# Transposes moved between TensorE and the DMA queue in a fused linear-attention and SwiGLU kernel

## The chip, the cores and the metric

The kernel runs on one core of one Trainium2 chip. The metric is the device time in microseconds of one execution; the median of several runs counts. A core has five engines with queues of their own: TensorE (PE in the profile; its weight loads are PEld), VectorE (DVE), ScalarE (ACT), GpSimd (POOL) and SyncE (SP), which here only issues DMAs. An engine takes its instructions strictly in the order in which the program lists them, so an instruction that waits holds up all that stands behind it on its engine.

## The reference

Eight batches of eight heads with 576 positions of 64 features go through a linear attention with cosine weights; its output, 4608 tokens of 512 features, goes through a normalized SwiGLU layer.

```python
def phi(x, c, s):
    r = np.maximum(x, 0.0)
    return np.concatenate([r * c, r * s], axis=-1)
q_p, k_p = phi(q, cos_w, sin_w), phi(k, cos_w, sin_w)
kv = np.einsum('bhsf,bhsd->bhfd', k_p, v)
z = np.sum(k_p, axis=2)
num = np.einsum('bhsf,bhfd->bhsd', q_p, kv)
den = np.einsum('bhsf,bhf->bhs', q_p, z)[..., None] + 1e-06
x = (num / den)                       # tokens x 512 after a transpose
xn = x / np.sqrt(np.mean(x * x, axis=-1, keepdims=True) + 1e-06) * rms_g
g, val = xn @ w_gate, xn @ w_val      # 512 -> 1536
out = (g / (1.0 + np.exp(-g)) * val) @ w_out
```

## The kernel before

**Blocks and tiles.** The tokens of a batch make a block: 512 of its 576 positions in four x tiles of 128 tokens. The last 64 positions of two batches each ("tails") make one further tile, and the four such tiles are block 8. The blocks of the SwiGLU layer run in the order 0, 1, 2, 3, 4, 5, 6, 8, 7. For a block there are twelve steps (n = 0 to 11), each with four matmuls of 512 columns for the gate into a bank `psG` and four for the value into a bank `psV` (`half_mm`, L528). `gval_h` then takes the silu of the gate on ScalarE (L547) and the product with the value on VectorE into `hT` (L548). Four output steps (n = 12 to 15) follow, of twelve matmuls each into `psC` (L551); their copies and stores are `out_store` (L562).

**From attention to an x tile.** For each batch, k, v and q are loaded into a ring of five `raw` buffers (`load_kv`, `load_q`; L109, L114, L123). `k_phi` and `q_phi` (L281 on ScalarE, L283 on VectorE) apply relu and the cosine or sine; `v_cast` makes v bf16; `kvz_pe` forms kv and z and `kvz_evac` saves them. The phi of q is transposed to `qpT`, by TensorE for batches 0 and 1 (`q_tr_pe`, L335), by a DMA transpose from SyncE for the others (`q_tr_dma`, L318). `nd_pe` (L421; `nd0_pe`, L430, in batch 0) forms numerator and denominator of one x tile in `psA`; `nd_post` on VectorE divides (reciprocal and L471); `x_sq` squares and sums on ScalarE (L487) and takes the power on GpSimd (L492, `rs`); `x_norm` on VectorE gives the normalized tile `xn` (L499). The tile must then be transposed into `xnT`, of which there are two, for even and odd blocks. For batches 0 and 1 TensorE does it: `x_tr_pe` (L518) makes four 128x128 transposes into a PSUM bank, and `x_tr_evac` copies that bank to `xnT` (L277 on VectorE, L275 on ScalarE). For the other batches SyncE issues a DMA transpose (`x_tr_dma`, L512).

**Queues and order.** The order on each engine is written out by hand. For the steady part it is a table: `at(block, step, where, f, ...)` puts a call into a slot, and `run` makes the calls of a slot before the matmuls of the step ("pe"), after them ("pre"), after the products ("post"), or amid the output matmuls ("mid"). Batch b+1's attention is thus made within block b. GpSimd issues the weight loads and, early in the program, loads of k, v and q; SyncE the others, with all stores and DMA transposes.

**The start of block 0.** To begin before all four x tiles exist, eight gate-and-value steps of block 0 are cut into eight `units`. A unit is (first tile, last tile, first n, last n): units 0 to 3 hold one tile and four n (sixteen matmuls of 128 columns for the gate, sixteen for the value), units 4 to 7 hold tiles 2 and 3 together and two n (eight matmuls of 256 columns for each). Unit i uses bank `psG[i % 2]` and `psV[i % 2]`; `unit_mm` (L618) makes its matmuls, `unit_silu` (L629) and `unit_h` (L633) its silu and product. `filler` (L573) multiplies zeros where TensorE would stand idle. The order written out there, around the change:

```python
    filler(2, psG[1])
    unit_mm(0, wg, by_rows=True)
    x_tr_pe(0, 1, psC[0])
    ...
    unit_mm(2, wg)
    x_tr_pe(0, 2, psC[1])
    x_tr_evac(V, 0, 2, psC[1])
    unit_silu(2)
    unit_h(0)
    unit_mm(3, wg)
    x_tr_pe(0, 3, psC[0])
    x_tr_evac(V, 0, 3, psC[0])
    unit_silu(3)
    unit_h(1)
    unit_mm(4, wg)
```

**The output stage of block 0.** `out_first` makes the 48 output matmuls of block 0, and amid them the four x tiles of batch 1 at the places of the table `X1`. For tile j that table lists where its `nd_pe`, its `x_norm` and its transpose go.

Of the kernel before, what the change touches and what calls it, by code (L numbers as in the profile page):

```python
# [17 lines left out]
def kernel(  # L18
# [11 lines left out]
    nc = tc.nc  # L30
# [3 lines left out]
    P = 128  # L34
# [6 lines left out]
    NDT = DM // P  # L41
# [5 lines left out]
    V, A, G = nc.vector, nc.scalar, nc.gpsimd  # L47
# [10 lines left out]
    psG = [ps.tile([P, 512], FP32, name=f"psG{i}") for i in range(2)]  # L58
    psV = [ps.tile([P, 512], FP32, name=f"psV{i}") for i in range(2)]
    psC = [ps.tile([P, 512], FP32, name=f"psC{i}") for i in range(2)]  # L60
# [66 lines left out]

    rqt = {}

    def load_q_tails(pair):  # L130
        rqt[pair] = two.tile([P, H, D], FP32, name="rqt", tag="rqt")
        for i in range(2):
            nc.sync.dma_start(
                out=rqt[pair][64 * i : 64 * i + 64, :, :],
                in_=q[2 * pair + i, :, 512:576, :].rearrange("h s d -> s h d"),
            )
# [31 lines left out]
    wg = one.tile([P, NDT, DFF], BF16, name="wg")  # L168
    wv = one.tile([P, NDT, DFF], BF16, name="wv")
# [42 lines left out]
    part, left = [], 1e-6  # L212
# [53 lines left out]
    xnT = [one.tile([P, NDT, TB], BF16, name=f"xnT{i}") for i in range(2)]  # L266
# [6 lines left out]
    def copy(eng, o, i):  # L273
        if eng is A:
            A.copy(out=o, in_=i)  # L275
        else:
            eng.tensor_copy(out=o, in_=i)  # L277
# [201 lines left out]
    def nd_post(b, j):  # L479
        nd_rec(b, j)  # L480
        nd_div(b, j)
# [22 lines left out]
    def x_dst(b, j):  # L504
        if j == 4:
            t, col = xnT_tail, b // 2
        else:
            t, col = xnT_of(b), j
        return t[:, :, col * P : (col + 1) * P]
# [4 lines left out]
    def x_tr_pe(b, j, bank, ts=(0, NDT)):  # L514
        xn = xn_of[(b, j)]
        dst = bank.bitcast(BF16).rearrange("p (t s) -> p t s", s=P)
        for t in range(*ts):
            nc.tensor.transpose(dst[:, t, :], xn[:, t * P : (t + 1) * P], ident[:, :])  # L518

    def x_tr_evac(eng, b, j, bank, ts=(0, NDT)):  # L520
        dst = bank.bitcast(BF16).rearrange("p (t s) -> p t s", s=P)
        copy(eng, x_dst(b, j)[:, ts[0] : ts[1], :], dst[:, ts[0] : ts[1], :])
# [48 lines left out]
    def filler(n, bank):  # L571
        for _ in range(n):
            nc.tensor.matmul(  # L573
                bank[:, :], lhsT=warm[:, 0:P], rhs=warm[:, :], start=True, stop=True
            )
# [30 lines left out]
    units = [(j, j + 1, 4 * i, 4 * i + 4) for i in range(2) for j in range(2)]  # L606
    units += [(2, 4, n, n + 2) for n in range(0, 8, 2)]
    sg_of = {}

    def unit_mm(i, w, by_rows=False):  # L610
        j0, j1, n0, n1 = units[i]
        bank = (psG if w is wg else psV)[i % 2]
        width = (j1 - j0) * P
        todo = [(n, t) for n in range(n0, n1) for t in range(NDT)]
        if by_rows:
            todo = [(n, t) for t in range(NDT) for n in range(n0, n1)]
        for n, t in todo:
            nc.tensor.matmul(  # L618
                bank[:, (n - n0) * width : (n - n0 + 1) * width],
                lhsT=w[:, t, n * P : (n + 1) * P],  # L620
                rhs=xnT[0][:, t, j0 * P : j1 * P],
                start=(t == 0 and (n == n0 or not by_rows)),
                stop=(t == NDT - 1 and (n == n1 - 1 or not by_rows)),
                skip_group_check=by_rows,
            )

    def unit_silu(i):
        sg_of[i] = four.tile([P, TB], FP32, name="sg", tag="sg")
        A.activation(out=sg_of[i][:, :], in_=psG[i % 2][:, 0:TB], func=AF.Silu)  # L629

    def unit_h(i):
        j0, j1, n0, n1 = units[i]
        V.tensor_tensor(  # L633
            out=hT[:, n0:n1, j0 * P : j1 * P],
            in0=psV[i % 2][:, 0:TB].rearrange("p (n s) -> p n s", n=n1 - n0),
            in1=sg_of[i][:, :].rearrange("p (n s) -> p n s", n=n1 - n0), op=ALU.mult,
        )
# [32 lines left out]
    q_tr_evac(A, 0, 3, qbank[3])  # L670
    x_norm(0, 1)
    nd_post(0, 2)
    filler(2, psG[1])
    unit_mm(0, wg, by_rows=True)
    x_tr_pe(0, 1, psC[0])
    x_tr_evac(V, 0, 1, psC[0])
    unit_mm(0, wv)
    x_sq(0, 2)
    load_wo(0, 4)
    unit_silu(0)  # L680
    nd0_pe(3)
    nd_post(0, 3)
    x_norm(0, 2)
    unit_mm(1, wg)
    unit_mm(1, wv)
    x_sq(0, 3)
# [6 lines left out]
    x_tr_evac(V, 0, 2, psC[1])  # L693
    unit_silu(2)
    unit_h(0)
    unit_mm(3, wg)
    x_tr_pe(0, 3, psC[0])
    x_tr_evac(V, 0, 3, psC[0])
    unit_silu(3)
    unit_h(1)  # L700
    unit_mm(4, wg)
    for i in range(2, 4):
        unit_mm(i, wv)
        unit_h(i)
    unit_silu(4)
    unit_mm(5, wg)
    unit_mm(4, wv)
    unit_silu(5)
# [4 lines left out]
    def at(blk, n, where, f, *args):  # L713
        slots.setdefault((blk, n), {}).setdefault(where, []).append((f, args))
# [19 lines left out]
    at(0, 10, "post", load_kv, "v", 2, (0, HP), G)  # L734
    at(0, 12, "pe", kvz_pe, 1)
    at(0, 12, "pe", kvz_evac, A, 1)
    at(0, 11, "post", load_q, 2, (0, 4), G)

    def x_tr(b, j, bank):
        x_tr_pe(b, j, bank)  # L740
# [3 lines left out]
    X1 = (  # L744
        ((12, "mid"), (13, "pe"), (14, "pe")),
        ((13, "pe"), (13, "mid"), (14, "mid")),
        ((13, "mid"), (14, "pe"), (15, "pe")),
        ((14, "pe"), (14, "mid"), (15, "mid")),
    )
# [3 lines left out]
        if j:  # L753
            at(0, *X1[j - 1][1], x_norm, 1, j - 1)
    at(0, *X1[3][1], x_norm, 1, 3)
    for j in range(4):
        at(0, *X1[j][2], x_tr, 1, j, psV[j % 2])
    for nb in range(2, B):
        b = nb - 1
        first = nb == 2  # L760
# [16 lines left out]
        for j in range(4):  # L777
            n = ((6, 8, 10, 12) if first else (4, 6, 8, 10))[j]
# [6 lines left out]
    for pair in range(4):  # L785
        b = 2 * pair or 3
        if pair == 0:
            at(1, 15, "post", load_q_tails, 0)
        at(b, 3, "post", q_tails_phi, V, pair, 0)
        at(b, 3, "post", q_tails_phi, A, pair, 1)  # L790
        at(b, 3, "post", q_tails_tr_dma, pair)
        at(b, 12, "pe", nd_tails_pe, pair)
        at(b, 12, "pre", nd_post, 2 * pair + 1, 4)
        at(b, 12, "post", x_sq, 2 * pair + 1, 4)
        at(b, 13, "post", x_norm, 2 * pair + 1, 4)
        at(b, 13, "post", x_tr_dma, 2 * pair + 1, 4)
    for nb in range(3, B):
        b = nb - 2
        late = b == 1
        at(b, 0, "post", load_kv, "k", nb)  # L800
        at(b, 5 if late else 3, "post", load_kv, "v", nb)
        at(b, 8 if late else 6, "post", load_q, nb)
        if nb % 2 == 1:
            at(b, 9, "post", load_q_tails, nb // 2)

    def gval_step(blk, n):
        run(blk, n, "pe")
# [86 lines left out]
```

## Time and profile before

| what | value |
|---|---|
| median of 3 runs | 325.12 us (324.64 to 325.19) |
| the profiled execution's own time | 324.66 us |
| its span, first to last instruction | 322.9 us |
| mean granted TensorE clock | 0.999 |
| busy share of the span: PE, PEld, DVE, ACT, POOL | 98%, 51%, 57%, 51%, 13% |
| DMA traffic | 53.37 MB, 165 GB/s on the mean |

All times inside an execution are counted from the start of the span, which is 1.8 us shorter than the execution's own time. A row of the timeline gives the start, the length, the engine with the source line, the operation, the tile written and the tiles read, their shapes, how many instructions were merged, and in brackets the idle time ahead and what ended it. A DMA's row is its issue (SPq for SyncE's queue); the data move later. Matmuls overlap: the length of a row holds the last one's way through the array, so the cost of a group is read from one start to the next.

In the 40 slices of the span the DMA engines are at 5 to 9 tenths in the first 27, and the granted TensorE clock is in the top tenth in every one.

### The profile page before, as it was taken

To read this page: it belongs to the slowest core of one execution; us is meant where nothing else is said; L and a number is where in the kernel's file an instruction comes from. 1 tells how busy PE (TensorE), PEld (TensorE's weight loads), DVE (VectorE), ACT (ScalarE), POOL (GpSimd) and SP (SyncE) were. 2 spreads that over 40 slices of the span, in tenths; PEclk is the share of its full clock that TensorE was granted. 3 is DMA by queue.
4 is the path that set the end of the run, shared out by engine and by line. 5 is a ranking of instruction groups with operands and counts; after the bars stand their busy time and mean duration, and the time that the engine had idled before them with its cause. 6 is when DMAs were issued, how large, how long until landed. Compare 5 with 4: busy or idle time off the path is not lost.

```text
span 322.9 us, 6078 instructions
## 1 busy us (share of the span) xinstructions
PE 315.6 (98%) x2312; PEld 163.5 (51%) x2348; DVE 185.5 (57%) x380; ACT 164.9 (51%) x319; POOL 40.6 (13%) x78
## 2 busy tenths in 40 slices
PE   8999999999999999999999999999999999999996
PEld 3688565544454445444544445444544444444444
DVE  8875958767636773676457745781577034204410
ACT  5664766744665457445754575446644333223321
POOL 9771302001001100011001000110011000000000
PEclk9999999999999999999999999999999999999999
DMA  7999996999789966998699959994822300041002
GB/s 229 233 266 272 283 327 240 230 200 240 149 156 232 234 190 161 195 233 202 175 198 214 210 148 207 202 217 141 119 49 48 117 32 0 2 98 31 3 32 97
DMA packets 77627, 53.37 MB, mean 165 GB/s; under 512 B 50410, under 2 KB 71326, under 8 KB 77598
## 3 DMA queue, kind: packets, MB, share of 16 engines
q1 hardware_dynamic: 70374, 39.81, 58.2%
q0 software_dynamic: 7216, 13.17, 16.5%
q8 instruction: 18, 0.29, 0.4%
q14 instruction: 11, 0.09, 0.1%
q10 hardware_dynamic: 8, 0.00, 0.0%
HBM read 37.83 MB, written 9.44 MB: 146 GB/s over the span
## 4 chain that ended last, share of the span: by engine, by line
PE 93%; DMA 2%; DVE 2%; issue 1%; POOL 0%; ACT 0%; ACTq 0%; POOLq 0%
PE psV L528 27%; PE psC L551 27%; PE psG L528 26%; PE psA L421 2%; DMA raw<-in_q_dram 2%; PE psG L551 2%; PE psV L618 2%; PE psA L359 2%; PE psG L618 1%; PE psA L366 1%; DVE xn L499 1%; PE psV L335 0%; PE psA L446 0%; DVE xt L471 0%; PE psG L402 0%
## 5 line engine op out<-in xcount | busy, mean ns | idle before, releaser
L548 DVE TENSOR_TENSOR hT<-psV,sg 128x512 bf16<-128x512 f32 x100 | 68.9, 689 | 102.1 <-PE psV L528 65.0
L547 ACT ACTIVATE sg<-psG 128x512 f32<-128x512 f32 x100 | 59.2, 592 | 62.5 <-PE psG L528 54.6
L528 PE MATMUL psV<-xnT,wv 128*128 128x512 bf16 x345 | 89.8, 379 | 0.6
L528 PE MATMUL psG<-xnT,wg 128*128 128x512 bf16 x338 | 88.6, 379 | 0.6 <-issue 0.2
L551 PE MATMUL psC<-wo,hT 128*128 128x512 bf16 (+1 forms) x398 | 88.6, 376 | 0.5
L551 PEld LDWEIGHTS <-hT 128*128 128x128 bf16 x456 | 42.9, 98 | 47.1
L528 PEld LDWEIGHTS <-wv 128*128 128x128 bf16 x400 | 39.1, 98 | 47.2
L528 PEld LDWEIGHTS <-wg 128*128 128x128 bf16 x400 | 37.0, 98 | 39.8
L492 POOL TENSOR_TENSOR rs<-ms,mhalf 128x1 f32<-128x1 f32 x36 | 19.8, 550 | 195.6 <-ACT scr L487 195.6
L275 ACT COPY osb<-psC 128x512 f32<-128x512 f32 x32 | 18.7, 585 | 50.0 <-PE psC L551 46.1
L487 ACT ACTIVATE scr<-xt 128x513 bf16<-128x513 f32 x36 | 22.8, 635 | 25.2 <-DVE xt L471 25.1
L499 DVE SCALAR_TENSOR_TENSOR xn<-xt,rs,gb 128x512 bf16<-128x512 f32 (+1 forms) x37 | 26.9, 730 | 10.3 <-POOL rs L492 10.3
L281 ACT ACTIVATE kp<-raw,tab 128x256 bf16<-128x256 f32 (+2 forms) x51 | 28.8, 607 | 2.3 <-DMA raw<-in_k_dram 2.3
L471 DVE TENSOR_TENSOR xt<-psA,rec 128x512 f32<-128x512 f32 x36 | 24.9, 692 | 1.2
L281 ACT ACTIVATE qp<-raw,tab 128x512 bf16<-128x512 f32 x32 | 22.6, 714 | 0.8 <-DMA raw<-in_q_dram 0.8
L283 DVE TENSOR_SCALAR kp<-raw,tab 128x256 bf16<-128x256 f32 (+2 forms) x53 | 20.4, 429 | 0.3 <-DMA raw<-in_k_dram 0.3
L283 DVE TENSOR_SCALAR qp<-raw,tab 128x512 bf16<-128x512 f32 x31 | 15.5, 506 | 0.3 <-DMA raw<-in_q_dram 0.3
L421 PEld LDWEIGHTS <-qpT 128*128 128x128 bf16 x224 | 10.5, 97 | 6.6 <-issue 0.5
L528 PE MATMUL psV<-xnT_tail,wv 128*128 128x512 bf16 x48 | 12.3, 379 | 0.1
L528 PE MATMUL psG<-xnT_tail,wg 128*128 128x512 bf16 x46 | 12.1, 379 | 0.1
L421 PE MATMUL psA<-kvzs,qpT 128*128 128x65 bf16 x224 | 11.4, 193 | 0.0
L277 DVE CAST vv<-raw 116x1280 bf16<-116x1280 f32 (+1 forms) x13 | 10.5, 807 | 0.0
(97 smaller groups left out, 181.2 us busy)
## 6 DMA issues: line engine op xcount, KB each, us to landing
out_dram<-osb SPq DMA_DIRECT2D x31, 256.0 KB, 2.4
raw<-in_k_dram SPq DMA_DIRECT2D x5, 1120.0 KB, 8.4
raw<-in_v_dram SPq DMA_DIRECT2D x5, 1120.0 KB, 8.5
raw<-in_q_dram SPq DMA_DIRECT2D x5, 1024.0 KB, 8.9
raw<-in_k_dram POOLq DMA_DIRECT2D x2, 1152.0 KB, 19.4
raw<-in_v_dram POOLq DMA_DIRECT2D x2, 1152.0 KB, 16.1
raw<-in_q_dram POOLq DMA_DIRECT2D x2, 1024.0 KB, 16.1
wg<-in_moe_w_gate_dram POOLq DMA_DIRECT2D x3, 512.0 KB, 14.2
```

The costliest lines, as they stand in the source:

```text
L275: A.copy(out=o, in_=i)
L281: A.activation(out=out_ap, in_=in_ap, func=AF.Relu, scale=scale)
L283: eng.tensor_scalar(out=out_ap, in0=in_ap, scalar1=scale, scalar2=0.0, op0=ALU.mult, op1=ALU.max)
L421: nc.tensor.matmul(heads[:, g, hp, :], lhsT=qpT[:, h, j * P : (j + 1) * P], rhs=kvzs[b][:, g, hp * E : (hp + 1) * E], start=True, stop=True,)
L471: V.tensor_tensor(out=xt[:, 0:DM].rearrange("p (hp g d) -> p g hp d", g=2, d=D), in0=heads[:, :, :, 0:D], in1=rec[:, :, :].unsqueeze(3).to ...
L487: A.activation(out=scr[:, :], in_=xt[:, 0 : DM + 1], func=AF.Square, scale=1.0 / math.sqrt(DM), accum_out=ms[:, :],)
L492: G.tensor_tensor(out=rs[:, :], in0=ms[:, :], in1=mhalf[:, :], op=ALU.pow)
L499: V.scalar_tensor_tensor(out=xn_of[(b, j)][:, c], in0=x_of[(b, j)][:, c], scalar=rs_of[(b, j)][:, :], in1=gb[:, c], op0=ALU.mult, op1=ALU. ...
L528: nc.tensor.matmul(bank[:, cols[0] : cols[1]], lhsT=w[:, t, n * P : (n + 1) * P], rhs=x[:, t, cols[0] : cols[1]], start=(t == 0), stop=(t ...
L547: A.activation(out=sg[:, :], in_=g[:, 0:TB], func=AF.Silu)
L548: V.tensor_tensor(out=hT[:, n, :], in0=v[:, 0:TB], in1=sg[:, :], op=ALU.mult)
L551: nc.tensor.matmul(bank[:, 0 : cols[1] - cols[0]], lhsT=hT[:, n, j * P : (j + 1) * P], rhs=wo[:, n, cols[0] : cols[1]], start=(n == 0), st ...
```

## The change

It has four parts.

1. In batch 0, x tile 3 is transposed after the first twelve of unit 3's sixteen gate matmuls rather than after all of them, and ScalarE evacuates it rather than VectorE, ahead of unit 3's silu. The gate of unit 4 is made one tile at a time by a new function, with sixteen matmuls of 128 columns: tile 2's eight at once, tile 3's eight behind the value of unit 2. The product of unit 2 then comes ahead of the silu of unit 4.
2. One filler of two ahead of unit 0 is left out.
3. In batch 1, x tiles 0 to 2 are transposed by DMA, issued by SyncE at each tile's `x_norm`; tile 3 stays on TensorE.
4. Loads: q of batch 2 is issued by SyncE behind the third of these transposes, not by GpSimd at (0, 11). Of batch 3, k goes from slot (1, 0) to (1, 4) and v from (1, 5) to (1, 6). The q tails of the first two pairs are issued by GpSimd, not by SyncE.

```diff
-    def load_q_tails(pair):
+    def load_q_tails(pair, eng=nc.sync):
...
-            nc.sync.dma_start(
+            eng.dma_start(
...
-    def unit_mm(i, w, by_rows=False):
+    def unit_mm(i, w, by_rows=False, part=(0, 16)):
...
-        for n, t in todo:
+        for n, t in todo[part[0] : part[1]]:
...
+    def unit_tile(i, j):
+        j0, j1, n0, n1 = units[i]
+        for n in range(n0, n1):
+            c = ((n - n0) * (j1 - j0) + j - j0) * P
+            for t in range(NDT):
+                nc.tensor.matmul(
+                    psG[i % 2][:, c : c + P], lhsT=wg[:, t, n * P : (n + 1) * P],
+                    rhs=xnT[0][:, t, j * P : (j + 1) * P],
+                    start=(t == 0), stop=(t == NDT - 1),
+                )
...
-    filler(2, psG[1])
+    filler(1, psG[1])
...
-    unit_mm(3, wg)
+    unit_mm(3, wg, part=(0, 12))
     x_tr_pe(0, 3, psC[0])
-    x_tr_evac(V, 0, 3, psC[0])
+    x_tr_evac(A, 0, 3, psC[0])
+    unit_mm(3, wg, part=(12, 16))
     unit_silu(3)
     unit_h(1)
-    unit_mm(4, wg)
-    for i in range(2, 4):
-        unit_mm(i, wv)
-        unit_h(i)
+    unit_tile(4, 2)
+    unit_mm(2, wv)
+    unit_h(2)
+    unit_tile(4, 3)
     unit_silu(4)
+    unit_mm(3, wv)
+    unit_h(3)
...
-    at(0, 11, "post", load_q, 2, (0, 4), G)
...
-    for j in range(4):
-        at(0, *X1[j][2], x_tr, 1, j, psV[j % 2])
+    for j in range(3):
+        at(0, *X1[j][1], x_tr_dma, 1, j)
+    at(0, *X1[3][2], x_tr, 1, 3, psV[1])
+    at(0, *X1[3][1], load_q, 2)
...
-            at(1, 15, "post", load_q_tails, 0)
+            at(1, 15, "post", load_q_tails, 0, G)
...
-        at(b, 0, "post", load_kv, "k", nb)
-        at(b, 5 if late else 3, "post", load_kv, "v", nb)
+        at(b, 4 if late else 0, "post", load_kv, "k", nb)
+        at(b, 6 if late else 3, "post", load_kv, "v", nb)
...
-            at(b, 9, "post", load_q_tails, nb // 2)
+            at(b, 9, "post", load_q_tails, nb // 2, G if nb == 3 else nc.sync)
```

(`late` holds for batch 3 alone.) On SyncE's queue the order behind the first two loads was: four stores, k of batch 3, four q transposes, v of batch 3. It becomes: three x transposes, q of batch 2, four stores, four q transposes, k of batch 3, v of batch 3. What follows keeps its order, but for the q tails.

## The prediction

> **What bounds the kernel.** I read the page first (busy shares, chain), then TensorE's waits, then the timeline around each edit.
>
> ```profile
> PE 315.6 (98%) x2312; PEld 163.5 (51%) x2348; DVE 185.5 (57%) x380; ACT 164.9 (51%) x319; POOL 40.6 (13%) x78
> ...
> PE 93%; DMA 2%; DVE 2%; issue 1%; POOL 0%; ACT 0%; ACTq 0%; POOLq 0%
> ```
>
> TensorE is busy for 98% and carries 93% of the chain. So time is won only by work taken off TensorE or by a stall that closes, and lost only by a new TensorE stall. The list of its waits has one that the change touches:
>
> ```profile
> PE psG L618 <- DVE xnT L277: 0.5, 1, 0.5
> ```
>
> The timeline shows where (first TensorE, then VectorE):
>
> ```profile
> 22.67 1.06 PE L618 MATMUL psG<-xnT,wg 128*128 128x128 bf16 x16
> 23.56 0.39 PE L518 MATMUL psC<-ident,xn 128*128 128x128 bf16 x4
> 24.48 1.05 PE L618 MATMUL psG<-xnT,wg 128*128 128x256 bf16 x8 [0.53 <-DVE xnT L277]
> 25.36 1.95 PE L618 MATMUL psV<-xnT,wv 128*128 128x128 bf16 x32
> ...
> 22.41 0.75 DVE L499 SCALAR_TENSOR_TENSOR xn<-xt,rs,gb 128x512 bf16<-128x512 f32 x1 [0.87 <-POOL rs L492]
> 23.07 0.42 DVE L277 COPY xnT<-psC 128x512 bf16<-128x512 bf16 x1
> 23.41 0.68 DVE L633 TENSOR_TENSOR hT<-psV,sg 128x512 bf16<-128x512 f32 x1
> 24.01 0.41 DVE L277 COPY xnT<-psC 128x512 bf16<-128x512 bf16 x1
> ```
>
> Tile 3 is transposed at 23.56, but VectorE evacuates it only at 24.01, behind a gate product; unit 4, which needs tiles 2 and 3, waits. The 0.53 is counted from a modelled matmul end. Sixteen 128-column matmuls start from 22.67 to 23.56, 0.056 each, so four transposes leave the array free at 23.78 and the loss is 24.48 - 23.78 = 0.69 us.
>
> **Part 1, batch 0, tile 3 and unit 4.** The transposes go four matmuls earlier, to 22.67 + 12 x 0.056 = 23.34; their input xn ends at 23.16, so they do not wait (0.13 us to spare after the semaphore, for which I take 0.05: tile 0's xn ends at 16.85 and its transposes start at 16.91). Then come the last four of unit 3 (to 23.78), eight for tile 2 alone (0.45, to 24.23; its copy ends at 23.49) and sixteen of unit 2's value (0.89, to 25.12). Tile 3's evacuation goes to ScalarE, which is free then: 0.57 (its 128x512 copy of batch 1) from about 23.78 to 24.35, hidden under these; the silu of unit 3 slips behind it to 24.86, and its bank is next written at 26.46. Unit 2's value needs its bank freed by the gate product of 23.41, which ends at 24.09: 0.09 us to spare, the thinnest point. Cost: unit 4's gate is sixteen matmuls of 0.056 (0.89) instead of eight that took 25.36 - 24.48 = 0.88, so 0.01 to 0.02. Unit 2's value comes 1.1 us earlier than before and needs the second part of wv, whose landing released GpSimd at 23.83; used at 24.23. Gain 0.67; between 0 (another wait takes its place) and 0.69.
>
> **Part 2, one filler less.** TensorE's timeline, then VectorE's xn of tile 1:
>
> ```profile
> 17.03 0.59 PE L573 MATMUL psG<-warm 128*128 128x512 bf16 x2
> 17.46 1.06 PE L618 MATMUL psG<-xnT,wg 128*128 128x128 bf16 x16
> 18.35 0.39 PE L518 MATMUL psC<-ident,xn 128*128 128x128 bf16 x4
> ...
> 17.52 0.75 DVE L499 SCALAR_TENSOR_TENSOR xn<-xt,rs,gb 128x512 bf16<-128x512 f32 x1
> ```
>
> It is worth 0.22 of TensorE, but tile 1's transposes, next but one, need the xn that ends at 17.52 + 0.75 = 18.27, a semaphore (0.05) before they now start. Unit 0 starts earlier and the transposes wait instead. I count 0.02; 0 to 0.1.
>
> **Part 3, batch 1's tiles 0 to 2 by DMA.** TensorE's timeline in block 0's output stage:
>
> ```profile
> 49.73 0.38 PE L518 MATMUL psV<-ident,xn 128*128 128x128 bf16 x4
> 49.95 1.46 PE L551 MATMUL psC<-wo,hT 128*128 128x512 bf16 x6
> 51.24 0.39 PE L518 MATMUL psV<-ident,xn 128*128 128x128 bf16 x4
> ...
> 54.28 0.39 PE L518 MATMUL psV<-ident,xn 128*128 128x128 bf16 x4
> ...
> 55.80 0.38 PE L528 MATMUL psG<-xnT,wg 128*128 128x512 bf16 x1
> ```
>
> Each removed set holds the array for 49.95 - 49.73 = 0.22: three are 0.67 us, in a stretch without a wait of over 0.2 us. The two ScalarE copies and the one VectorE copy that go with them lay beside matmuls. The Trainium skill ("TensorE: Matmul & The Clock Gate", Part 4) gives about 275 ns for one transpose in a kernel; by that the twelve would be 3.3 us. The rows decide: 219 ns is how long one lasts, 0.056 is what it takes from the next.
>
> What takes their place: VectorE finishes xn of tile 2 at 51.79, less part 1's 0.69 is 51.1; SyncE then issues for 1.2 us, and with an empty ring a tile lands 2.4 to 2.5 us after its issue starts (the late xnT issues): 53.6. Block 1 now begins at 55.80; less 0.69 and 0.67 is 54.44. So 0.8 us to spare. Tile 3 keeps TensorE; its VectorE copy ended at 55.43, and with one copy fewer ahead ends 0.33 earlier, while the start comes 0.67 earlier: the 0.37 of slack becomes 0.03, less a semaphore: cost 0.03, at most 0.1.
>
> **Part 4, the loads.** The issues that move or that decide, GpSimd's and SyncE's:
>
> ```profile
> 38.59 0.77 POOL L109 DMA_DIRECT2D raw<-in_v_dram  x1
> 39.35 0.90 POOL L123 DMA_DIRECT2D raw<-in_q_dram  x1
> ...
> 57.17 1.00 SPq L114 DMA_DIRECT2D raw<-in_k_dram  x2
> 68.63 1.09 SPq L114 DMA_DIRECT2D raw<-in_v_dram  x2
> 72.87 1.21 SPq L512 DMA_TRANSPOSE xnT<-xn  x1
> ```
>
> q of batch 2 leaves GpSimd's queue at 39.35 (it landed 15.3 later, 54.6) for SyncE's, behind the third transpose: issue at about 52.4. Batch 3's q, a megabyte, passed in 3.1 us (77.0 to 80.1 in the packets), so with 1.3 us from issue to its first packet (v of batch 3: issue 68.63, first packet 69.9) and half a microsecond to land it is there near 57.5. Its first reader, ScalarE's phi, stood at 59.88, less 1.36 is 58.5: 1 us to spare, and behind that the silu of unit 2 has some 3 us before TensorE wants its bank. The four stores of block 0 queue behind q; nobody waits for them soon. Cost 0.
>
> k of batch 3 goes from 57.17 to behind batch 2's four q transposes (last at 67.29, less 1.36, plus 1.2: 67.2), v behind it, then the x tile, q and so on. The issue of k and v took 8.4 to 8.5 us to land; back to back k lands near 75, v 80 to 81, q 3 us after the x tile behind v, 83.5 to 84.5. Their first readers (81.29, 84.58 and 85.71, less 1.36) ask at 79.9, 83.2 and 84.4, so VectorE may stand for q a little, in a stretch where it idles 4 us afterwards. Behind q stand two x tiles (consecutive ones landed 0.5 apart), two stores (about 0.7 of packets each) and batch 2's last tile: 86.8 to 88.3, while block 2, now at 89.22, wants it at 87.9. I take no stall; bounds 0 and 1.0. The q tails go to GpSimd, two issues of about 0.8 us each time, between rs steps more than 3 us apart: nothing, though their 256 KB cross the same engines.
>
> **Sum.** 0.67 + 0.02 + 0.67 - 0.03 = 1.33 us; I take 1.3. Span 322.9 to 321.6; profiled execution 324.66 to 323.4. That lies 0.46 under the median of the runs, so the median goes from 325.12 to 323.8.
>
> **Rivals.** (a) Batch 2's last x tile lands late behind k, v, q and stores, which now go out within 7 us (67 to 74) where they were spread over 17 (57 to 74). For: no row has all three loads so close, and SyncE stood up to 4.3 us on a transpose behind loads. Against: it needs the upper half of my landings. Price 0.3 to 1.0: 324.1 to 324.8.
>
> (b) One of part 1's thin covers fails (the bank of unit 2's value, 0.09): half of the 0.67 or all returns as another wait: 324.2 to 324.5.
>
> (c) Slower: batch 1's tiles reach block 1 late because v of batch 2 still fills the DMA engines (issued 38.59, landed 13.1 later, at 51.7), while tiles 0 and 1 are issued at 47.7 and 49.4. It decides once tile 2 lands after 54.44, and makes the kernel slower than before once that is past 55.8. For: transposes behind loads in one ring landed after 4.8 to 9.4 us, which from 51.1 is 55.9 to 60.5, a loss of 0.1 to 4.7 net. Against: those stood behind whole loads; here v is in another queue and gone by 51.7, and three tiles need 1.5 us of empty engines: 53.7. Time 325.2 to 329.8. The Trainium skill ("DMA: Bandwidth & Descriptors", Queues, rings and completion order) speaks for (c): an engine goes round its queues packet by packet, so a tile's 256-byte pieces would each wait for a large one of v. No row here shows transposes beside that queue.
>
> (d) The change does nothing measurable: parts 1 and 3 both replaced by waits; 325.1.
>
> **Chances.** Forecast 0.62, (a) 0.16, (b) 0.08, (c) 0.08, (d) 0.06. A measurement of this kernel can tell about 0.2%, 0.65 us: faster is the forecast, (b) and two thirds of (a), some 0.79; same 0.12; slower 0.09. The range reaches from 323.2 (no evacuation cost, filler at its bound, and the runs' spread of 0.5 below) to 325.2, which leaves out most of (c).
>
> **What would show it.** Right: the wait on xnT in unit 4 gone, no L518 between 48 and 53, block 1's first matmul near 54.4 without a wait, block 2's near 87.9. Wrong: a TensorE wait on DMA xnT at either block start (rivals c, a), one on a gate product near 24.2 (b), or the q phi of batch 2 standing on its load beyond 60.

## The result, and the profile after

The changed kernel takes 334.26 us (median of 6 runs, 332.05 to 337.34), the kernel before 324.94 beside it (324.39 to 325.19): a ratio of 1.0281, 95% interval 1.0235 to 1.0327. It is 9.3 us slower by these medians, where 1.3 us of gain were forecast. One of the six runs (337.34) counts as slow and is left out of the ratio; the median of the other five is 333.50, 8.6 us above the kernel before, and differences of medians below go by it. The profiled execution took 336.15 us, its span 334.4.

The page first: TensorE's share, the granted clock in 40 slices (8.36 us each), and the shares of the chain that ended last.

```profile
PE 319.4 (96%) x2343; PEld 163.4 (49%) x2343; DVE 184.9 (55%) x378; ACT 164.8 (49%) x318; POOL 42.5 (13%) x81
...
PEclk9999999999958999999999999999999999999999
...
PE 89%; DMA 6%; POOL 2%; issue 1%; DVE 1%; SPq 0%; ACT 0%; POOLq 0%; ACTq 0%
```

TensorE fell from 93% to 89% of the chain and DMA rose from 2% to 6%; in the 12th and 13th slices the clock is down to 5 and 8 tenths. TensorE's list of waits has one new head (total, times, longest, in us), and unit 4's wait on `xnT` is gone from it:

```profile
PE psG L528 <- DMA xnT<-xn: 10.3, 1, 10.3
```

TensorE's timeline at the four places that the prediction named (unit 4 in batch 0, tile 3 of batch 1, the starts of blocks 1 and 2; L633 is here the new `unit_tile`):

```profile
23.07 0.39 PE L518 MATMUL psC<-ident,xn 128*128 128x128 bf16 x4
...
24.02 1.07 PE L618 MATMUL psV<-xnT,wv 128*128 128x128 bf16 x16
24.92 0.61 PE L633 MATMUL psG<-xnT,wg 128*128 128x128 bf16 x8
...
52.72 0.39 PE L518 MATMUL psV<-ident,xn 128*128 128x128 bf16 x4
...
54.27 1.04 PE L528 MATMUL psG<-xnT,wg 128*128 128x512 bf16 x4
...
77.34 10.52 PE L551 MATMUL psC<-wo,hT 128*128 128x512 bf16 x48
98.18 1.86 PE L528 MATMUL psG<-xnT,wg 128*128 128x512 bf16 x4 [10.31 <-DMA xnT<-xn]
99.83 1.91 PE L528 MATMUL psV<-xnT,wv 128*128 128x512 bf16 x4
101.54 1.91 PE L528 MATMUL psG<-xnT,wg 128*128 128x512 bf16 x4
103.25 1.12 PE L528 MATMUL psV<-xnT,wv 128*128 128x512 bf16 x4
```

Up to 87.9 everything runs as forecast: no wait in unit 4, block 1 at 54.27 without one, and block 2 could begin at 98.18 - 10.31 = 87.87 (before: 89.22), a gain of 1.35. Then TensorE stands for 10.31 us on batch 2's last x tile. The next four groups of four matmuls take 1.65, 1.71, 1.71 and 0.95 from start to start (to L359 at 104.20), 6.02 in all; four at the 0.86 to 0.87 of block 1 are 3.46. So a half-speed clock (0.50 in the window 98 to 102 below) costs 2.56 more. 10.31 + 2.56 - 1.35 = 11.5, which is the whole difference of the spans (334.4 - 322.9).

SyncE's issues ahead of that wait (start, length of the issue):

```profile
67.13 1.11 SPq L114 DMA_DIRECT2D raw<-in_k_dram  x2
68.34 1.39 SPq L114 DMA_DIRECT2D raw<-in_v_dram  x2
71.36 1.25 SPq L512 DMA_TRANSPOSE xnT<-xn  x1
72.70 0.53 SPq L123 DMA_DIRECT2D raw<-in_q_dram  x1
75.10 9.11 SPq L512 DMA_TRANSPOSE xnT<-xn  x2
84.30 1.53 SPq L562 DMA_DIRECT2D out_dram<-osb  x2
85.93 2.79 SPq L512 DMA_TRANSPOSE xnT<-xn  x1
```

From the trace's landings: k 74.6, v 81.4, the first x tile 83.7, q 90.5, the others 94.2, 96.6 and 98.1. GpSimd issued the q tails at 73.8, 74.5, 81.9 and 82.6; they landed at 85.5, 86.5, 96.0 and 96.4. The windows show that the DMA engines had work all the time and moved little (columns: length; busy time of PE, PEld, DVE, ACT and POOL with counts; clock; DMA share, which is over 1 where packets overlap; GB/s):

```profile
78.00:82.00 4.00, 4.00 (x20) 1.86 (x19) 2.58 (x7) 1.86 (x5) 0.58 (x2) 1.00 1.34 82
...
86.00:90.00 4.00, 1.87 (x9) 0.66 (x7) 0.00 (x0) 0.52 (x1) 0.00 (x0) 1.00 1.65 141
90.00:94.00 4.00, 0.00 (x0) 0.00 (x0) 2.01 (x4) 2.43 (x4) 0.00 (x0) 0.90 1.17 97
94.00:98.00 4.00, 0.00 (x0) 0.10 (x1) 0.00 (x0) 0.00 (x0) 0.00 (x0) 0.50 1.05 216
98.00:102.00 4.00, 3.82 (x10) 1.34 (x10) 0.14 (x1) 1.21 (x2) 0.00 (x0) 0.50 0.82 207
```

From 78 to 82, with v and q queued, 82 GB/s were moved, and 97 from 90 to 94; in the kernel before the stretch 78 to 82 moved 289.

### The profile page after: what moved, and what is told of

Read it like the earlier page. It is cut to its first block, busy times and chain, and to the rows that moved or that the text cites. A ratio compares the mean times of both kernels' runs of the same rounds, so it can differ in the third digit from the quotient of the medians.

```text
span 334.4 us, 6110 instructions
## 1 busy us (share of the span) xinstructions
PE 319.4 (96%) x2343; PEld 163.4 (49%) x2343; DVE 184.9 (55%) x378; ACT 164.8 (49%) x318; POOL 42.5 (13%) x81
## 4 chain that ended last, share of the span: by engine, by line
PE 89%; DMA 6%; POOL 2%; issue 1%; DVE 1%; SPq 0%; ACT 0%; POOLq 0%; ACTq 0%
PE psG L528 26%; PE psV L528 26%; PE psC L551 24%; DMA xnT<-xn 4%; DMA raw<-in_q_dram 2%; PE psV L618 2%; PE psA L421 2%; PE psG L551 2%; PE psG L618 2%; PE psA L359 2%; PE psA L366 1%; POOL qp L283 1%; PE psV L335 0%; PE psA L446 0%; SPq L562 0%
## 5 line engine op out<-in xcount | busy, mean ns | idle before, releaser
L528 PE MATMUL psG<-xnT,wg 128*128 128x512 bf16 x352 | 92.1, 385 | 10.3 <-DMA xnT<-xn 10.3
L528 PE MATMUL psV<-xnT,wv 128*128 128x512 bf16 x352 | 91.3, 382 | 0.0
L283 DVE TENSOR_SCALAR qp<-raw,tab 128x512 bf16<-128x512 f32 x31 | 14.7, 479 | 6.5 <-DMA raw<-in_q_dram 6.5
## 6 DMA issues: line engine op xcount, KB each, us to landing
raw<-in_v_dram POOLq DMA_DIRECT2D x2, 1152.0 KB, 16.1
```

The lines of the kernel that those rows point to most:

```text
L283: eng.tensor_scalar(out=out_ap, in0=in_ap, scalar1=scale, scalar2=0.0, op0=ALU.mult, op1=ALU.max)
L528: nc.tensor.matmul(bank[:, cols[0] : cols[1]], lhsT=w[:, t, n * P : (n + 1) * P], rhs=x[:, t, cols[0] : cols[1]], start=(t == 0), stop=(t ...
```

## The experiments

Two theories at first: the backlog (k, v, q, x tiles and stores back to back in SyncE's queue make the last tile late, rival (a) with a higher price) and the tails (on GpSimd they cross that backlog and slow it). Edits are against the changed kernel unless said otherwise; medians stand beside 324.8 to 325.4 for the kernel before, measured with each, and ratios are to it. The tails are called by the step of block 1 at which they are issued: the step-9 pair goes out first, the step-15 pair second (the expectations call now one, now the other the first pair).

**e1: both tail pairs back on SyncE.**

```diff
-            at(1, 15, "post", load_q_tails, 0, G)
+            at(1, 15, "post", load_q_tails, 0)
...
-            at(b, 9, "post", load_q_tails, nb // 2, G if nb == 3 else nc.sync)
+            at(b, 9, "post", load_q_tails, nb // 2)
```

> The changed kernel with the q tails of the first two pairs issued by SyncE again; k, v of batch 3 stay late. Theory T (the q tails in GpSimd's queue and SyncE's transposes hold each other up): the 10.3 us wait ahead of block 2 goes, q of batch 3 lands near 85 rather than 90.5, about 323.6 us, as predicted blind. Theory L (k, v and q of batch 3 follow each other too closely in SyncE's ring): the wait stays, 331 us or more, since nothing of these loads changes. Theory TL (either alone is harmless): about 323.6 us.

326.46 us (325.51 to 328.04), ratio 1.0051 (1.0029 to 1.0073): between theories T and L. TensorE's timeline at block 2's start:

```profile
90.15 1.25 PE L528 MATMUL psG<-xnT,wg 128*128 128x512 bf16 x4 [2.28 <-DMA xnT<-xn]
```

So 7.0 of the 8.6 us come with two lines that I had put at nothing; the backlog alone leaves a wait of 2.28, and in this profiled run (327.49) a slow clock after it (0.61 from 90 to 94) that takes another 1.7:

```profile
90.00:94.00 4.00, 3.85 (x11) 1.48 (x12) 0.79 (x2) 1.21 (x2) 0.00 (x0) 0.61 1.01 233
```

Not every run of e1 has it: eight of the twelve had a mean clock of 0.998 to 1.000 and took 325.51 to 326.58, four had 0.995 and took 327.49 to 328.04. The DMA rate tells the two kernels apart, in 40 slices of 0.825 us from 66 to 99, first the changed kernel:

```profile
GB/s 139 162 167 68 348 284 268 278 264 183 216 254 264 254 246 99 20 67 57 108 271 178 151 200 327 291 99 19 15 174 12 43 136 114 56 283 327 111 319 261
```

and e1:

```profile
GB/s 139 150 185 53 320 290 239 262 242 197 168 275 270 310 259 124 23 225 346 350 360 153 6 166 170 220 335 311 337 251 360 235 163 161 150 7 209 170 146 340
```

Both have a hole at slice 17 (79.2), where v ends and the first x tile is transposed. In e1 it is one slice, q follows at 350, and a second hole of one slice comes where q ends (84.2). With the tails on GpSimd, whose packets begin at 79, it is four slices, and two more holes come at 87 to 90 and 91 to 92, with the step-15 pair.

**e2: k and v of batch 3 at their old slots, tails left on GpSimd.**

```diff
-        at(b, 4 if late else 0, "post", load_kv, "k", nb)
-        at(b, 6 if late else 3, "post", load_kv, "v", nb)
+        at(b, 0, "post", load_kv, "k", nb)
+        at(b, 5 if late else 3, "post", load_kv, "v", nb)
```

> The changed kernel with k and v of batch 3 at their former places, the q tails still on GpSimd. T: the tails still meet the x transposes of batch 2, so a wait of several us ahead of block 2 stays: 328 to 334 us. L: about 323.6 us. TL: about 323.6 us.

328.29 us (325.92 to 330.4), ratio 1.0089 (1.0061 to 1.0117). That lies in theory T's range, but not by T's wait: the one on `xnT` is gone, and another stands in its place:

```profile
PE psA L421 <- DMA qpT<-qp: 3.0, 1, 3.0
```

q of batch 2, four stores and k now stand ahead of batch 2's q transposes: the first is issued at 60.31 and lands at 69.56. So with q of batch 2 on SyncE, k and v could not stay where they were; moving them exchanged one late transfer for another.

**e3: the tails alone**, on GpSimd in the kernel before (the reverse of e1's edit there).

> The kernel before with only the q tails of the first two pairs moved to GpSimd. T: slower by several us, 328 to 334 us, with a TensorE wait on DMA xnT at block 2. L and TL: 325 us, no such wait.

325.09 us, ratio 0.9998 (0.9978 to 1.0019), and no wait on `xnT` at block 2 in the list. The first load of the step-9 pair was issued at 75.16 and landed at 82.03, after q (80.75). Without the backlog the tails on GpSimd cost no time, so my zero would have held for the queue of before. But they did cost a landing: batch 2's last x tile came at 89.32 rather than 87.71, and block 2, which began at 89.22 before, at 89.41. The slack of 1.5 us hid the price.

**e4: k, v and tails as before; parts 1 to 3 stay, and q of batch 2 on SyncE** (e1's and e2's edits together).

> The changed kernel with the q tails and k, v of batch 3 as before: what is left are the order in batch 0, one filler less, three x tiles by DMA and q of batch 2 on SyncE. All of T, L and TL: no wait ahead of block 1 or block 2, 323.6 us (1.3 us under the kernel before). If it is slower than 325, the loss has another part in parts 1 to 3.

328.43 us (326.11 to 330.15), ratio 1.0091 (1.0057 to 1.0126); the wait on `qpT` is 4.0. It differs from e2 by the tails alone and takes the same time, so there too the tails on GpSimd cost nothing that shows; the 323.6 that all three theories gave missed the wait on `qpT`.

**e5: all loads as before; parts 1 to 3 stay.** Also:

```diff
+    at(0, 11, "post", load_q, 2, (0, 4), G)
...
-    at(0, *X1[3][1], load_q, 2)
```

> Every load as before the change (q of batch 2 on GpSimd again, k and v of batch 3 early, tails on SyncE); batch 0's order, the filler and three x tiles of batch 1 by DMA as in the change. Theory R (the whole loss is the crowding of SyncE's ring by the moved loads; parts 1 to 3 are as worked out): 323.6 us, no wait at block 1. Theory X (an x tile by DMA does not land while a load of GpSimd's queue is under way; here q of batch 2 goes on until about 54.6): a TensorE wait on DMA xnT ahead of block 1 of 0.5 to 2 us, 324.1 to 326.

326.21 us (325.34 to 327.05), ratio 1.0038 (1.0023 to 1.0052). Rival (c)'s wait, from the list of waits:

```profile
PE psG L528 <- DMA xnT<-xn: 1.7, 1, 1.7
```

The three tiles were issued at 47.58, 49.27 and 50.98 and landed at 55.15, 55.63 and 56.05, all behind q of batch 2, which GpSimd had issued at 39.70 and which landed at 54.69. The DMA rate from 44 to 60 in slices of 0.4 us:

```profile
GB/s 385 393 438 415 392 392 392 403 426 369 369 403 380 365 372 397 329 369 328 321 289 202 34 140 93 113 210 236 310 410 292 241 266 92 87 102 282 307 213 289
```

q alone moves some 390. The tiles' first 256-byte packet starts at 51.80, 4.2 us after the first issue, and q's 4 KB packets run on beside them until 54.14; from 52.8 to 54.4 the two together move 34 to 140. So q had to leave GpSimd's queue, and that started the rest.

**e6: part 1 and 2 alone** (e5, and all four x tiles of batch 1 on TensorE again). **e10: the same with both fillers.**

> Of the change only batch 0's order and one filler less; batch 1's x tiles on TensorE, every load as before. Theory R and X both: the wait of 0.5 on the evacuation of tile 3 is gone and nothing takes its place, 0.65 to 0.7 us under the kernel before, 324.2 us. If that gain is covered by the next wait: 324.9 us.

> Of the change only batch 0's order; both fillers stay. Blind working: 0.67 us under the kernel before, 324.3 us, and 0.02 above the same with one filler less. If the filler is worth its 0.22 after all: 0.2 us above the run of both parts (which lay 0.93 under the kernel before).

e6: 324.06 us, ratio 0.9969 (0.9957 to 0.998). e10: 324.02, ratio 0.997 (0.9958 to 0.9981). The new order in batch 0 is worth 0.9 by the medians and 0.5 to 0.6 by the spans (322.4 and 322.3, against 322.9); the filler nothing.

**e7: part 3 alone**, in the kernel before.

```diff
-    for j in range(4):
-        at(0, *X1[j][2], x_tr, 1, j, psV[j % 2])
+    for j in range(3):
+        at(0, *X1[j][1], x_tr_dma, 1, j)
+    at(0, *X1[3][2], x_tr, 1, 3, psV[1])
```

> The kernel before with only x tiles 0 to 2 of batch 1 transposed by DMA. R: 0.67 us under the kernel before, 324.2 us. X: tile 2 is issued at 51.8 while q of batch 2 fills the engines until 54.6, and block 1 wants it at 55.1: no wait or a wait of up to 2 us, 324.2 to 326.5 us; tile 0 lands more than 5 us after its issue.

326.48 us, ratio 1.0047 (1.0031 to 1.0062). The tiles landed at 56.00, 56.48 and 56.90, again right behind q (55.49), and block 1 began at 57.04 (before: 55.80):

```profile
57.04 1.02 PE L528 MATMUL psG<-xnT,wg 128*128 128x512 bf16 x4 [0.68 <-ACT kp L281]
```

The landings confirm e5 without part 1. The loss of time does so less: the profile puts this wait down to a phi of k on ScalarE, which ended together with the last tile, and in this run (327.03) TensorE had already lost 1.1 us to a wait on q's phi early in the program (before: 0.2).

**e8: the step-9 pair of tails on SyncE. e14: the step-15 pair on SyncE.**

> The changed kernel with the first pair of tails it loads, issued at step 9, on SyncE again; the other, issued at step 15, stays on GpSimd. Theory S (a GpSimd load held up behind SyncE's full ring and the x transposes behind it slow one another): if the pair at step 9 does the harm, most of the 8 us go and it is near 326.5 us, as with both back; if the pair at step 15 does it, 333 us stays; if each does its part, between, 329 to 331 us.

> The changed kernel with the first pair of tails (step 15) back on SyncE, the second (step 9) still on GpSimd; the mirror of e8. After is 334.3, e8 330.7, both pairs back 326.5. If the two pairs cost independently, the first one's return takes back 3.6 and this gives 330 to 331. If the second pair does harm only because the first has already made a backlog, it gives 326.5 to 328. If the second alone makes all of it, 333 to 334, and e8's 330.7 does not fit.

e8: 330.71 us, ratio 1.018 (1.016 to 1.0199), wait 4.1. e14: 331.65 us, ratio 1.0193 (1.0164 to 1.0223), wait 6.4. Against e1 (326.46) the step-15 pair on GpSimd (e8) costs 4.3 and the step-9 pair (e14) 5.2, both together 7.0: less than the sum, but neither needs the other. These medians hold the slow clock too (mean 0.989 to 0.995 in all runs of e8 and e14, near 1 in most of e1). The wait alone, in one profiled run each, grows from 2.28 by 1.8 with the step-15 pair, by 4.1 with the step-9 pair and by 8.0 with both, more than the sum.

GpSimd also reaches the tails earlier than SyncE, which is a rival to the queue itself: in e1 SyncE issues the step-15 pair at 91.7, behind the last x tile, GpSimd in e8 at 81.9, ahead of it. A pair ahead of that tile in SyncE's own queue takes 1.54 us of landings in e1 (0.87 and 0.67 for its two loads), so the place alone could explain the 1.8. It does not explain the step-9 pair, which lies ahead of the tile in both: in e14 v landed 3.0 us later than in e1, the first x tile 3.9 and q 6.1 (0.4 of each from a later issue).

**e9: does a tail pair slow a transpose by itself?** Kernel before; GpSimd loads a tail pair that nobody reads at four steps of block 6, where SyncE has only x transposes.

```diff
+    def probe():
+        for i in range(2):
+            G.dma_start(out=prb[64 * i : 64 * i + 64, :, :],
+                        in_=q[i, :, 512:576, :].rearrange("h s d -> s h d"))
+    for n in (5, 7, 9, 11):
+        at(6, n, "post", probe)
```

> The kernel before with four added loads of a q tail pair (256 KB each, into a buffer that nobody reads), issued by GpSimd in block 6 just ahead of the DMA transposes of batch 7's x tiles, where the DMA engines have nothing else to do. The transposes land 2.4 us after their issue in the kernel before. Theory X (a transpose does not move while a load of GpSimd's queue is under way, and goes on at full speed once it is done): each lands 0.2 to 0.6 us behind the end of its load, at 3 to 5 us after issue. Theory S (the two slow one another): load and transpose both take longer than one behind the other, 6 us or more, as in the changed kernel. If the queues take turns without loss: 2.4 to 3.5 us. TensorE has 3.7 us and more of slack there, so the time stays at 325 us in all but the second case.

325.08 us, ratio 1.0005 (0.9995 to 1.0015). The transposes landed 2.59 to 3.06 us after their issue (2.4 before), each 0.4 to 0.6 behind the pair. Their packets begin 1.2 to 1.5 us after the issue (1.2 before) and 0.2 to 0.7 before the pair's last ends. So the two hardly met, and together they lost 0.2 to 0.7 us, within the range given for queues that take turns without loss; the several us that theory S asked for do not come from a pair and a lone transpose.

**e13 and e17: the same pair amid loads and transposes**, in the quiet stretch of the kernel before (from 260 on). SyncE issues a list of 1 MB loads L and 128 KB transposes T.

```diff
...
+    at(8, 0, "post", probe, 0, "LLTLTT", False)      # e13
+    at(8, 11, "post", probe, 11, "LLTLTT", True)     # pair on GpSimd at once
+    at(7, 6, "post", probe, 6, "LLL", True)
...
+    at(8, 0, "post", probe, 0, "LLTLTT", True)       # e17: pair on GpSimd 4.6 us later
+    at(8, 11, "post", probe, 11, "LLTLPTT", False)   # P: pair on SyncE
+    at(7, 6, "post", probe, 6, "LLLL", True)         # pair late
```

> The kernel before, with three groups of idle transfers added where its DMA engines are quiet (block 8 and 7), whose results nobody reads; a group is a list of SyncE issues, L a megabyte of q and T a 128 KB transpose. Group 1: L L T L T T, no tail pair. Group 2: the same, with one tail pair on GpSimd ahead. Group 3: L L L with a tail pair. By the rows of before a lone L lands about 8.5 us after its issue and others 3 to 4 us behind it, a T 0.5 to 2.4 us behind what is ahead: group 1 should end 18 to 22 us after its first issue. Theory mixed (a GpSimd load beside a ring that holds both loads and transposes makes the engines slow): group 2 ends at least 4 us later than group 1, group 3 within 1.5 us of three loads (15 to 17 us). Rival, loads alone suffice: group 3 is late by 4 us too. Rival, it needs something of block 1 that these groups lack (stores, the engines' loads on SBUF): group 2 within 1.5 us of group 1.

> The kernel before, with idle transfers in its quiet stretch as in e13 (L a megabyte of q, T a 128 KB transpose, both on SyncE; P a tail pair on SyncE, in the list). Group 1: L L T L T T, with the pair on GpSimd some 4.6 us later, so that its packets meet the first T and the third L. Group 2: L L T L P T T, the pair in SyncE's own queue. Group 3: L L L L with the late pair on GpSimd, no transposes. In e13 L L T L T T without a pair ended 13.3 us after its first issue, with the early pair on GpSimd 15.2, and L L L with it 13.2. The pair's own bytes are 0.8 us at 350 GB/s, a fourth L 3.0. Theory transposes (two queues collapse when a transpose stands in one of them): group 1 ends at 18 us or later, group 2 at 14.0 to 14.5, group 3 at 16 to 17. Rival, any two busy queues lose about a microsecond: group 1 at 15 to 16, group 3 at 16 to 17. Rival, it needs block 1's other work: group 1 within 0.5 of group 2.

From first issue to last landing: e13 13.3, 15.2 and 13.2 us; e17 16.1, 15.0 and 17.4. Both theories of a collapse fell: transposes are not needed (in e17's third group the rate falls to 168 to 242 GB/s too), and nothing near 4 us is lost. e17's two figures with the pair on GpSimd lie 0.1 and 0.4 above the ranges of the rival that any two busy queues lose about a microsecond. By one run, a pair on GpSimd costs 1.2 us more than the same pair in SyncE's queue. Where it goes is seen in e17's first group (40 slices of 0.2 us from 270 to 278):

```profile
GB/s 195 55 22 339 369 174 358 374 374 282 215 169 205 246 138 282 108 220 169 143 215 164 220 210 179 179 241 348 348 298 292 274 50 101 292 249 83 0 0 0
```

From 272 to 275.2 the pair's packets and L's alternate, and the two together move some 190 GB/s where L alone moved 350.

**e18: one pair at the same place of block 5**, in the kernel before, whose queue has k, v, an x tile and q close together there.

```diff
-            at(b, 9, "post", load_q_tails, nb // 2)
+            at(b, 6 if nb == 7 else 9, "post", load_q_tails, nb // 2, G if nb == 7 else nc.sync)
```

> The kernel before with its last tail pair issued by GpSimd at step 6 of block 5, behind q of batch 7, where SyncE's queue holds k, v, an x tile and q close together as in block 1 of the changed kernel (before: issued 195.8 to 205.3; q landed 214.2, the last x tile 218.6, needed at 223.8). If the place makes the cost, q lands at 217.5 or later and the last x tile past 221; if a pair costs what it does in the quiet stretch, q lands at 215 to 216.5 and the last x tile by 220. No change of the time is expected by either, since 5 us are to spare: within 0.5 of before.

325.93 us in one run (beside 324.88), 1.05 more where at most 0.5 was expected; span 324.1. q landed 6.9 us behind v (212.2 to 219.2) where it was 3.7 (210.5 to 214.2), so the pair cost q 3.2; k and v were themselves 1.7 late, as they were issued 1.9 later, for a reason not settled. The last x tile landed at 220.5 rather than 218.6, hardly later than that shift, since the pair was out of its way by then. This lies between the two expectations: more than in the quiet stretch, less than the last tile lost in block 1.

**e11, e12, e16, e15: can the change be mended?** e11 is e1 with k of batch 3 at step 2; e12 also moves the step-9 pair, on SyncE, to step 13; e16 is e11 with both pairs on GpSimd; e15 is e12 with only tiles 0 and 1 by DMA. The lines of e12 (its step-15 pair is as in e1):

```diff
-        at(b, 4 if late else 0, "post", load_kv, "k", nb)
+        at(b, 2 if late else 0, "post", load_kv, "k", nb)
...
-            at(b, 9, "post", load_q_tails, nb // 2, G if nb == 3 else nc.sync)
+            at(b, 13 if late else 9, "post", load_q_tails, nb // 2)
```

> The changed kernel with the q tails on SyncE and k of batch 3 at step 2 of block 1 instead of 4, between the second and third q transposes. Theory C (the 2.3 us wait that is left with the tails back comes from SyncE's ring running on without a break from k to the last x tile, so that an earlier start of k ends it earlier): k goes out about 3.4 us earlier, the last x tile of batch 2 lands before 87.8, no wait at block 2: 323.6 us. Against C: the wait moves to the third q transpose, which stands behind k (needed at 73.4): 324 to 326 us.

> As the kernel with k at step 2, and the first pair of tails goes behind the last x tile of batch 2 (step 13 rather than 9). C: the ring is 1.2 us shorter ahead of the last x tile; if k at step 2 alone leaves no wait the time is the same, 323.6 us; if it leaves a wait, this is up to 1.2 us faster.

> e11 (324.7: the changed kernel, tails on SyncE, k of batch 3 at step 2) with both pairs of tails on GpSimd, as the change has them. If the tails do harm because k, v, q and the x tiles are one backlog, k's being out of it leaves less: between 325 and 329. If v, q and the tiles suffice, 331 to 334, as in the changed kernel. If the tails were only delayed behind k, within 0.5 of e11.

> e12 (323.9: k at step 2, tails on SyncE, second pair at step 13) with only tiles 0 and 1 of batch 1 by DMA; tile 2 stays on TensorE, and q of batch 2 is issued one tile earlier. TensorE gets four transposes back (+0.22), all of SyncE's queue behind moves about 1.2 to 1.7 us forward. If the queue at block 2 still limits (e12 has a wait of 0.6 there), 323.4 to 323.9; if it does not, 324.1 to 324.3.

e11: 324.72 us, ratio 1.0001 (0.9988 to 1.0015), wait 0.7: theory C in part, as the earlier k takes 1.6 off e1's wait and not all of it. e12: 323.89 us (323.59 to 324.11), ratio 0.9962 (0.995 to 0.9975), the lowest median here, ahead of the kernel before and of the changed one, though not to be told from part 1 alone (e6, e10: 324.0 to 324.1). Its block 2 still waits a little, and keeps its clock:

```profile
88.47 1.02 PE L528 MATMUL psG<-xnT,wg 128*128 128x512 bf16 x4 [0.64 <-DMA xnT<-xn]
```

e16: 327.55 us (325.55 to 332.75), ratio 1.0069 (1.0042 to 1.0096), wait 3.8: with k out of the backlog the tails on GpSimd cost 2.8 over e11, not 7.0. So their price grows with what is queued. e15: 324.42 us, ratio 0.9989 (0.998 to 0.9998): above either range expected: the wait stays (0.8), and the third tile by DMA is worth its place.

## Why the prediction was wrong

**Part 1 was right.** The wait in unit 4 is gone, nothing took its place (24.02, then 24.92 without a wait), and e10 has 0.5 to 0.9 for it where 0.67 was worked out. **Part 2** was worth nothing, as its bounds allowed.

**Part 3 was right where the queue allows it.** Tile 2 landed at 53.34 (53.6 worked out), block 1 began at 54.27 (54.44), block 2 could have begun at 87.87 (87.9), and up to there 1.35 were gained of the sum's 1.33. e12 keeps most of it: 322.9 - 322.3 + its wait of 0.64 = 1.24.

**Part 4 failed**, first of all in the step "The q tails go to GpSimd ... nothing, though their 256 KB cross the same engines." The text said that they share the engines and still priced them at their issue on GpSimd alone. The runs give 7.0 us (after against e1) for what is 512 KB in all. e8 and e14 give 4.3 to 5.2 for each pair. The text also left out that GpSimd would issue them up to 10 us earlier. The second step that failed is "I take no stall; bounds 0 and 1.0" for batch 2's last x tile: with the tails back it still left 2.28 (e1).

The landings of the rest were nearly right. In e1, k came at 74.8 (75 worked out), v at 80.4 (80 to 81), q at 85.5 (83.5 to 84.5), the last x tile at 90.1 (86.8 to 88.3); of its excess the two tail loads, which e1 has ahead of it, take 0.87 and 0.67. q landed 4.5 behind the x tile, not 3. The holes of 23 and 6 GB/s at the ends of v and of q, where a transpose stands behind a load, were not in the estimate. The kernel before has such holes too (46, 23 and 18 GB/s for 1.3 us at the end of v in block 5); I had not looked for them in the rate.

**Rival (a) was the right kind, with its price too low.** It said 0.3 to 1.0; the last tile was 2.28 late in e1 and 10.31 in the changed kernel. It also priced the wait alone. In the profiled runs a stall of 2.28 was followed by 1.7 of slow clock, one of 10.31 by 2.56.

**Rival (c)** described e5 and e7, not the changed kernel: there v landed at 51.40, the tiles at 51.91, 52.33 and 53.34, in time. Its rule from the Trainium skill ("DMA: Bandwidth & Descriptors", Queues, rings and completion order), that an engine goes round its queues packet by packet, agrees with the traces where two queues met: in e5 the tiles' packets and q's ran side by side from 51.80 to 54.14, in e17 a load's and a pair's from 272 to 275.2, at 190 GB/s together. In e5 the tiles' first packet came 4.2 us after the issue, in e7 2.4, in the changed kernel, beside v, 1.3; what held the first two up no run shows.

**What stays open.** That tails on GpSimd cost the time, some 4 to 5 us for each pair alone, and less with a smaller backlog, is shown. Why a pair costs that in block 1, 3.2 of q's landing in block 5 and 1.2 in the quiet stretch is not. Nor is it shown how much of the step-15 pair's price is its earlier place rather than its queue: no run has it on SyncE ahead of the last x tile. The holes of 12 to 70 GB/s lie where an x tile is transposed while the pair's packets are under way; whether it is that meeting was not isolated, since e17, which put the three together, showed only the 190.

## What to carry to other kernels

A load moved to an idle engine's queue is moved off that engine's time, not off the DMA engines: price it at the place where it will run, by what is queued there. A run with the load alone moved (e3) shows no price in its time where slack hides it; read the landings too. When transfers are pushed together to free one of them, list every landing up to the next one that TensorE needs, and add the slow clock to the price of a stall. In e12 the loss went away with three things together: the tails in SyncE's queue, k of batch 3 two steps earlier, and the step-9 pair behind the last x tile.

## What the runs showed of the hardware that I had not expected

- Transposes of SyncE beside a 1 MB load of GpSimd's queue: first packet 4.2 us after the issue, the two together at 34 to 140 GB/s where the load alone moved 390, and the first tile landed 0.46 behind the load (e5).
- A pair of 256 KB on GpSimd's queue beside SyncE's 1 MB loads brings both together to some 190 GB/s, from 350 (e17).
- After 2.28 us without work TensorE's granted clock was 0.61 over the next four (e1); after 10.31 it was 0.50 from 94 to 102 and four matmuls took 1.71 rather than 0.87. Waits of 1.7 (e5), 0.64 (e12) and 3.8 (e16) left it at 1.00, and eight of e1's twelve runs show a mean clock of 0.998 or more, so the length alone does not decide.
- With loads queued ahead SyncE stood on the issue of one transpose for up to 6.9 us (e14; the 9.11 at 75.10 in the changed kernel are two); alone an issue takes 1.2.
